# Loading the first block of tokens in two halves, one on each DMA queue

## The chip, the core and the metric

The kernel runs on one core of a Trainium2 chip. A core has five engines with instruction queues of their own: TensorE (matmuls; PE in the profile), VectorE (DVE), ScalarE (ACT), GpSimd (POOL) and SyncE (SP). SyncE and ScalarE also issue the transfers between the chip's main memory (HBM) and the on-chip memory (SBUF); matmul results go to PSUM, from where VectorE or ScalarE must copy them before their bank can be used again. The metric is the device time of one execution in microseconds (us), the median of several.

## What is computed

One transformer layer with two branches in parallel: attention over a window of 256 keys with 32 heads of 16 channels, and a bilinear feed-forward part. Both read the same layer norm of x; x is 2048 tokens by 512 channels in bf16.

```python
def _A_ref(x, wqkv, wo):
    H = 32; Dh = D // H; W = 256
    qkv = transpose((x @ wqkv).reshape(B, S, 3, H, Dh), 2, 0, 3, 1, 4)
    q, k, v = qkv[0], qkv[1], qkv[2]
    scores = jnp.einsum("bhqd,bhkd->bhqk", q, k) * (Dh ** -0.5)
    mask = (idx[:, None] - idx[None, :] >= 0) & (idx[:, None] - idx[None, :] < W)
    p = _softmax(jnp.where(mask[None, None], scores, -1e9), axis=-1)
    return transpose(jnp.einsum("bhqk,bhkd->bhqd", p, v), ...).reshape(B, S, D) @ wo

def _B_ref(x, w_gate, w_up, w_down):
    h = jnp.einsum("bsd,df->bsf", x, w_gate) * jnp.einsum("bsd,df->bsf", x, w_up)
    return jnp.einsum("bsf,fd->bsd", h, w_down)

xn = _layernorm(x, axis=-1)
return x + _A_ref(xn, A_wqkv, A_wo) + _B_ref(xn, B_w_gate, B_w_up, B_w_down)
```

## The kernel before

The tokens are cut into 16 blocks of 128 (x0 to x15) and the work into four chunks of four blocks. A planner in the kernel's own Python code decides, while the program is built, in which order the pieces of work are put on the engines. It is given constants for how long each piece takes, and for when each load is expected to land (`land` for the blocks of x, `wv`, `wk`, `wq` for the thirds of Wqkv). These constants do nothing on the chip: they only set the order, and which of two engines takes a copy.

The loads are issued at the head of the program:

```python
def qkv(eng, lo, k0, k1):     # 512 of the 1536 columns of Wqkv, rows k0 to k1 of 4 slices of 128
    load(eng, self.Wqkv[:, k0:k1, lo:lo + 512], w["qkv"][:, k0:k1, lo:lo + 512])

load(nc.scalar, self.x[:, 0, :], xv[:, 0, :])
load(nc.sync, self.x[:, 1, :], xv[:, 1, :])
qkv(nc.sync, 1024, 0, 2)      # V weights, k 0,1
qkv(nc.scalar, 1024, 2, 4)    # V weights, k 2,3
qkv(nc.scalar, 512, 2, 4)     # K weights, k 2,3
qkv(nc.sync, 512, 0, 2)       # K weights, k 0,1
load(nc.sync, self.x[:, 2, :], xv[:, 2, :])
qkv(nc.sync, 0, 0, 4)         # Q weights
load(nc.sync, self.x[:, 3, :], xv[:, 3, :])
# ... then, all on nc.sync: Wg and Wu in halves, x4 to x7, x8 to x15
for f, g in ((0, 5), (5, 10), (10, 14)):
    load(nc.sync, self.Wd[:, f:g], w["d"][:, f:g])
load(nc.sync, self.Wo[:], w["o"])
for _ in range(4):
    nc.sync.drain()
# ... small constants; a Sqrt of one element on ScalarE brings in its table:
nc.scalar.activation(out=warm[:], in_=warm[:], func=ACT.Sqrt)
# ...
for _ in range(4):
    nc.vector.drain()
self.keep_busy(42, 0)         # 42 matmuls of 128 columns on constants
```

The first chunk, block by block (b = 0 to 3), with what each step needs:

```python
land = (3.35, 3.4, 7.5, 9.6)
wv, wk, wq = 5.6, 6.9, 9.2
# st{b}: bn_stats and bn_aggr of x[b]          VectorE, after the load of x[b]
# sq{b}: sqrt(var + eps)                       ScalarE
# rs{b}: reciprocal                            VectorE
# ap{b}: xn[b] = (x - mean) * rs               VectorE, block 0 in two halves of 256 channels
def turn(i, ks, b=b):                        # TensorE: four 128x128 transposes into PSUM
    for k in ks:
        self.nc.tensor.transpose(self.psT(i)[:, k, :], self.xn[b][:, 128 * k:128 * k + 128], self.ident[:])
    if b == 0:
        self.keep_busy(2 * ks[0], 3)
# xT{b}: copy to xnT[0] in SBUF                ScalarE or VectorE
def project(i, lo, tok=tok):                 # K (lo = 512) and Q (lo = 0) of one block: 16 matmuls
    for k in range(4):
        for c in range(4):
            self.nc.tensor.matmul(
                self.M[i][:, 128 * c:128 * c + 128], lhsT=self.Wqkv[:, k, lo + 128 * c:lo + 128 * c + 128],
                rhs=self.xnT[0][:, k, tok], start=k + c == 0, stop=k == 3, skip_group_check=True)
# V of one block: 16 matmuls too; then the copies out of PSUM (K in two, Q and V in one)
```

TensorE works in the order it is given. In the first chunk that is: the 42 matmuls, the transposes of block 0, V of block 0, the transposes of block 1, K of block 0, K of block 1, Q of block 0, the transposes of block 2, and so on; then the feed-forward part, the scores and the values in turns until the end.

Of the kernel before, what the change touches and what calls it, by code (L numbers as in the profile page):

```python
# [90 lines left out]
class Kernel:  # L91
# [58 lines left out]
    def prologue(self):  # L150
        nc = self.nc
        xv = self.x_d.rearrange("(t p) d -> p t d", p=128)
        w = {k: v.rearrange("(k p) n -> p k n", p=128) for k, v in self.w_d.items()}

        def load(eng, dst, src):
            eng.dma_start(out=dst, in_=src)

        def qkv(eng, lo, k0, k1):
            load(eng, self.Wqkv[:, k0:k1, lo:lo + 512], w["qkv"][:, k0:k1, lo:lo + 512])

        load(nc.scalar, self.x[:, 0, :], xv[:, 0, :])
        load(nc.sync, self.x[:, 1, :], xv[:, 1, :])
        qkv(nc.sync, 1024, 0, 2)
        qkv(nc.scalar, 1024, 2, 4)
        qkv(nc.scalar, 512, 2, 4)
        qkv(nc.sync, 512, 0, 2)
        load(nc.sync, self.x[:, 2, :], xv[:, 2, :])
        qkv(nc.sync, 0, 0, 4)
        load(nc.sync, self.x[:, 3, :], xv[:, 3, :])
        h = self.F // 2  # L170
        for lo in (0, h):
            load(nc.sync, self.Wg[:, :, lo:lo + h], w["g"][:, :, lo:lo + h])
            load(nc.sync, self.Wu[:, :, lo:lo + h], w["u"][:, :, lo:lo + h])
            if lo == 0:
                load(nc.sync, self.x[:, 4:8, :], xv[:, 4:8, :])
        load(nc.sync, self.x[:, 8:NT, :], xv[:, 8:NT, :])
        for f, g in ((0, 5), (5, 10), (10, 14)):
            load(nc.sync, self.Wd[:, f:g], w["d"][:, f:g])
        load(nc.sync, self.Wo[:], w["o"])
        for _ in range(4):  # L180
            nc.sync.drain()

        c = self.const
        nc.gpsimd.memset(self.ident[:], 0.0)
        nc.gpsimd.affine_select(out=self.ident[:], in_=self.ident[:], compare_op=ALU.not_equal, fill=1.0,
                                base=0, pattern=[[-1, 128]], channel_multiplier=1)
        nc.gpsimd.memset(self.mhalf[:], -0.5)
        warm = c.tile([128, 1], F32, name="warm")
        nc.vector.memset(warm[:], 0.0)
        nc.vector.memset(self.eps[:], 1e-5)  # L190
        nc.scalar.activation(out=warm[:], in_=warm[:], func=ACT.Sqrt)
        self.warm = warm
        pi = c.tile([128, 1], I32, name="pi")
        nc.gpsimd.iota(pi[:], pattern=[[0, 1]], base=0, channel_multiplier=1)
        podd = c.tile([128, 1], I32, name="podd")
        nc.vector.tensor_scalar(out=podd[:], in0=pi[:], scalar1=4, scalar2=1,
                                op0=ALU.arith_shift_right, op1=ALU.bitwise_and)
        nc.vector.tensor_copy(out=self.own[:, 1:2], in_=podd[:])
        nc.vector.tensor_scalar(out=self.own[:, 0:1], in0=podd[:], scalar1=0, scalar2=None, op0=ALU.is_equal)
        nc.gpsimd.memset(self.V[0][:, :, :, 16:18], 1.0)  # L200
        for _ in range(4):
            nc.vector.drain()
        self.keep_busy(42, 0)


# [385 lines left out]

    def first_chunk(self):

        land = (3.35, 3.4, 7.5, 9.6)
        wv, wk, wq = 5.6, 6.9, 9.2
        nc = self.nc
        roots = []
        for b in range(4):
# [36 lines left out]
        for b in range(4):  # L635
# [40 lines left out]
            for n, ks in enumerate(([0, 1], [2, 3]) if b == 0 else ([0, 1, 2, 3],)):  # L676
                self.A.insert(at + n, Dense(f"turn{b}", 1.1 * len(ks) / 4, [("ap", b, n)], lambda i, f=turn, ks=ks: f(i, ks),
                                            lambda o, i, f=turned, ks=ks: f(o, i, ks)))
# [172 lines left out]
```

The softmax here doesn't subtract the row's maximum and nothing guards it: scores larger than these inputs give would overflow.

## Time and profile before

| what | value |
|---|---|
| time, median of 3 | 264.75 us (264.62 to 264.78) |
| profiled execution | 903.53 us, span 901.7 us |
| TensorE busy | 897.7 us of the span |
| ScalarE, VectorE, GpSimd busy | 168.1, 195.0, 118.1 us |
| HBM read and written | 9.70 and 2.10 MB |

In the profiled execution TensorE worked far more slowly than in the timed ones (42 matmuls of 128 columns take 8.67 us at its head), so its durations are not those of the 264.75 us; the times of loads, VectorE and ScalarE do not hang on TensorE's speed except where they wait for it. A line of a timeline reads: start, duration, engine (q for the queue that issues a transfer), source line, operation, output <- input, how many, and in brackets the idle time before it and what ended it. A line of the DMA view gives output <- input, issuing queue, count, size of one, and us from issue to landing.

### The profile page before, as it was taken

Reading aid. Unit: us, or ns where it says so; the run is one execution under the profiler, and the core shown is the slowest. Engines: PE = TensorE matmul, PEld = TensorE weight load, DVE = VectorE, ACT = ScalarE, POOL = GpSimd, SP = SyncE. Lnnn points to the kernel's source line nnn. Section 1 sums busy time; section 2 is a strip of 40 time slices with the busy share of each in tenths; the row PEclk is TensorE's granted clock in tenths of the full one; section 3 lists DMA queues with packets and bytes.
Section 4 is the critical chain, followed back from the end, with each engine's and each line's share of the span. In section 5 each row is a group of like instructions: output and inputs, shape, how many; then the busy total and the mean of one; then the engine's idle time right before and its main releaser. Section 6 shows DMA issues by size and latency. Waiting matters only on the chain.

```text
span 901.7 us, 8001 instructions
## 1 busy us (share of the span) xinstructions
PE 897.7 (100%) x3456; PEld 290.7 (32%) x3456; DVE 195.0 (22%) x367; ACT 168.1 (19%) x122; POOL 118.1 (13%) x274
## 2 busy tenths in 40 slices
PE   9999999999999999999999999999999999999998
PEld 8832223523222222343222222324323232322333
DVE  2132222222222021312222021312202022222101
ACT  2221112222112121121121211111212121120000
POOL 0112111210212011110212011110110202011000
DMA  9301000000001000000000000000000000000000
GB/s 328 104 0 24 0 1 1 0 1 1 1 6 24 12 7 0 1 1 1 0 18 19 6 7 0 1 1 1 1 4 8 6 1 7 1 0 0 1 1 24
DMA packets 17252, 13.89 MB, mean 15 GB/s; under 512 B 7104, under 2 KB 17216, under 8 KB 17216
## 3 DMA queue, kind: packets, MB, share of 16 engines
q1 hardware_dynamic: 16384, 12.65, 4.7%
q10 hardware_dynamic: 832, 0.72, 0.2%
q8 instruction: 27, 0.44, 0.2%
q14 instruction: 9, 0.07, 0.0%
HBM read 9.70 MB, written 2.10 MB: 13 GB/s over the span
## 4 chain that ended last, share of the span: by engine, by line
PE 100%; DVE 0%; issue 0%; DVEq 0%
PE M L221 75%; PE S L229 7%; PE M L259 7%; PE M L707 6%; PE M L655 3%; PE M L211 1%; PE S L221 1%; PE M L640 0%; DVE xn L801 0%; DVEq L801 0%
## 5 line engine op out<-in xcount | busy, mean ns | idle before, releaser
L512 ACT ACTIVATE P<-S 128x2048 bf16<-128x2048 f32 x75 | 140.8, 1877 | 459.0 <-PE S L229 452.7
L238 POOL TENSOR_SCALAR_AFFINE_SELECT P<-P 64x256 bf16<-64x256 bf16 (+1 forms) x250 | 111.0, 446 | 673.9 <-ACT P L512 662.8
L221 PE MATMUL M<-xnT,Wu 128*128 128x512 bf16 x224 | 197.7, 1114 | 0.0
L221 PE MATMUL M<-xnT,Wg 128*128 128x512 bf16 x224 | 194.0, 1056 | 0.0
L221 PE MATMUL M<-Wd,hT 128*128 128x512 bf16 (+1 forms) x224 | 181.9, 1056 | 0.0
L221 PEld LDWEIGHTS <-Wg 128*128 128x128 bf16 x224 | 44.4, 204 | 119.1 <-issue 119.1
L221 PEld LDWEIGHTS <-Wu 128*128 128x128 bf16 x224 | 42.5, 197 | 121.9 <-issue 121.9
L221 PEld LDWEIGHTS <-hT 128*128 128x128 bf16 x238 | 45.2, 198 | 112.7 <-issue 112.1
L221 PE MATMUL M<-xnT,Wqkv 128*128 128x512 bf16 x96 | 79.8, 1085 | 0.0
L759 DVE TENSOR_TENSOR hT<-M,gsb 128x512 bf16<-128x512 f32 x56 | 38.7, 691 | 172.8 <-PE M L221 172.8
L229 PE MATMUL S<-Q,K 32*128 32x320 bf16 (+4 forms) x720 | 67.9, 532 | 0.0
L259 PE MATMUL M<-P,V 64*17 64x320 bf16 (+4 forms) x1440 | 62.1, 591 | 0.0
L217 DVE CAST gsb<-M 128x512 bf16<-128x512 f32 x44 | 30.4, 691 | 139.5 <-PE M L221 139.5
L229 PEld LDWEIGHTS <-K 32*128 32x128 bf16 x720 | 16.4, 115 | 122.5 <-issue 121.7
L221 PE MATMUL M<-Wo,OT 128*128 128x512 bf16 (+1 forms) x64 | 53.8, 1070 | 0.0
L707 PE MATMUL M<-Wqkv,xnT 128*64 128x256 bf16 x256 | 53.1, 670 | 0.0
L259 PEld LDWEIGHTS <-V 64*17 64x17 bf16 x1440 | 42.2, 188 | 22.2 <-issue 18.0
L550 DVE STREAM_TRANSPOSE at<-M 128x512 f32<-128x512 f32 x32 | 21.5, 699 | 85.3 <-PE M L259 85.3
L707 PEld LDWEIGHTS <-xnT 128*64 128x64 bf16 x256 | 33.9, 209 | 18.6 <-issue 10.8
L801 DVE TENSOR_TENSOR y<-M,x 128x512 bf16<-128x512 f32 x12 | 8.3, 691 | 121.0 <-PE M L221 121.0
L221 PEld LDWEIGHTS <-Wqkv 128*128 128x128 bf16 x96 | 18.1, 196 | 50.8 <-issue 50.8
L655 PE MATMUL M<-xnT,Wqkv 128*128 128x128 bf16 x128 | 27.2, 484 | 0.0
(53 smaller groups left out, 211.7 us busy)
## 6 DMA issues: line engine op xcount, KB each, us to landing
Wg<-in_B_w_gate_dram SPq DMA_DIRECT2D x2, 896.0 KB, 9.5
Wu<-in_B_w_up_dram SPq DMA_DIRECT2D x2, 896.0 KB, 11.3
out_dram<-y SPq DMA_DIRECT2D x12, 128.0 KB, 1.7
Wd<-in_B_w_down_dram SPq DMA_DIRECT2D x2, 640.0 KB, 12.9
x<-in_A_x_dram SPq DMA_DIRECT2D x1, 1024.0 KB, 14.3
Wqkv<-in_A_wqkv_dram ACTq DMA_DIRECT2D x2, 256.0 KB, 5.2
Wqkv<-in_A_wqkv_dram SPq DMA_DIRECT2D x2, 256.0 KB, 4.8
Wqkv<-in_A_wqkv_dram SPq DMA_DIRECT2D x1, 512.0 KB, 6.7
```

The lines of the kernel that those rows point to most:

```text
L211: self.nc.tensor.matmul(self.M[i][:, 0:128], lhsT=ones, rhs=ones, start=True, stop=True)
L217: self.nc.vector.tensor_copy(out=out, in_=in_)
L221: self.nc.tensor.matmul(ps, lhsT=a, rhs=b, start=first and n == 0, stop=last and n == len(pairs) - 1)
L229: self.nc.tensor.matmul(self.S[:, e, 64 * at:64 * (at + m)], lhsT=self.K[U % 3][rows, c, j].rearrange("p l t -> p (l t)"), rhs=self.Q[T % ...
L238: self.nc.gpsimd.affine_select(out=v, in_=v, pattern=[[0, 4], [0, n], [sign, 64]], base=0, fill=0.0, compare_op=ALU.is_gt if kind else ALU ...
L259: self.nc.tensor.matmul(banks[lane][32 * e:32 * e + 17, 64 * q:64 * (q + m)], lhsT=self.V[U % 3][rows, j, 4 * c + e, 0:17], rhs=P[rows, e, ...
L512: ex = self.op(f"exp{g}", {"A": (took + 0.06, took + 0.18)}, [o], lambda e: self.nc.scalar.activation(out=P[:, :, 0:hi], in_=self.S[:, :, ...
L550: t = self.op(f"tr{v}", {"V": (0.63, 0.71)}, [o] + ts, lambda e, par=par: nc.vector.transpose(out=self.at[:, :, par, :], in_=self.M[banks[ ...
L655: self.nc.tensor.matmul(self.M[i][:, 128 * c:128 * c + 128], lhsT=self.Wqkv[:, k, lo + 128 * c:lo + 128 * c + 128], rhs=self.xnT[0][:, k, ...
L707: self.nc.tensor.matmul(self.M[i][64 * lane:64 * lane + 64, 256 * jj:256 * jj + 256], lhsT=self.xnT[T % 2][:, k, tok], rhs=w[:, lane], sta ...
L759: x = self.op(f"u{T}.{f}", {"V": PSUM_COPY["V"]}, [o, ("gate", T, f)], lambda e: self.nc.vector.tensor_tensor(out=self.hT[T % 2][:, f, :], ...
L801: self.nc.vector.tensor_tensor(out=keep["y"][:, cols], in0=self.M[i][:, cols], in1=self.x[:, t, cols], op=ALU.add)
```

## The change

The first block of x, which everything else waits for, is cut into two halves of 64 tokens (64 partitions). Each of the two queues that issue loads starts with one half, so that no other load stands ahead of x0 or beside it. The load of x1, which stood at the head of SyncE's queue, goes behind the half of x0 on ScalarE's queue, ahead of the weights. The other loads keep their order; Wd is loaded in two parts, not three; three of four drains of VectorE are left out. The planner is given new landing times to match.

```diff
-        load(nc.scalar, self.x[:, 0, :], xv[:, 0, :])
-        load(nc.sync, self.x[:, 1, :], xv[:, 1, :])
+        load(nc.sync, self.x[0:64, 0, :], xv[0:64, 0, :])
+        load(nc.scalar, self.x[64:128, 0, :], xv[64:128, 0, :])
+        load(nc.scalar, self.x[:, 1, :], xv[:, 1, :])
         qkv(nc.sync, 1024, 0, 2)
         qkv(nc.scalar, 1024, 2, 4)
         qkv(nc.scalar, 512, 2, 4)
@@
-        for f, g in ((0, 5), (5, 10), (10, 14)):
+        for f, g in ((0, 7), (7, 14)):
             load(nc.sync, self.Wd[:, f:g], w["d"][:, f:g])
@@
-        for _ in range(4):
-            nc.vector.drain()
+        nc.vector.drain()
         self.keep_busy(42, 0)
@@
-        land = (3.35, 3.4, 7.5, 9.6)
-        wv, wk, wq = 5.6, 6.9, 9.2
+        land = (3.25, 3.9, 7.7, 9.7)
+        wv, wk, wq = 5.9, 7.3, 9.4
```

## The prediction

> **What bounds the kernel now.** I read the page's busy shares and chain first. The profiled execution is 901.7 us long against 264.75 us timed, so the first question is which of its numbers may be used.
>
> ```profile
> span 901.7 us, 8001 instructions
> ...
> PE 897.7 (100%) x3456; PEld 290.7 (32%) x3456; DVE 195.0 (22%) x367; ACT 168.1 (19%) x122; POOL 118.1 (13%) x274
> ...
> DMA  9301000000001000000000000000000000000000
> ...
> PE 100%; DVE 0%; issue 0%; DVEq 0%
> ```
>
> The chain of work is TensorE from end to end, so here every wait of the head is hidden behind a slow TensorE. In the chain in order of time, 48 projection matmuls of 128 columns take 9.77 us, 204 ns each. Timed, all of 901.7 us of such work has to fit in 264.75 - (903.53 - 901.7) = 262.9 us, so TensorE is at least 3.4 times faster there. I therefore take TensorE's order from the profile, but not its durations. Durations of VectorE, ScalarE and the transfers I take as they stand. The DMA row matters next: it is busy in the first two slices (45 us) and then nearly nothing, so this change can act on the head alone.
>
> The timeline of the first 6 us, from issue of the loads to the first normalised tile (start, duration, engine and line, what ended the wait):
>
> ```profile
> 0.80 0.41 ACTq L156 DMA_DIRECT2D x<-in_A_x_dram  x1
> ...
> 0.80 0.40 SPq L156 DMA_DIRECT2D x<-in_A_x_dram  x1
> ...
> 2.28 1.28 ACT L191 ACT_TABLE_LOAD   x1 [2.28 <-issue]
> ...
> 3.58 0.20 ACT L191 ACTIVATE warm<-warm 128x1 f32<-128x1 f32 x1
> ...
> 3.61 0.69 DVE L607 BATCH_NORM_STATS2 st<-x 128x6 f32<-128x512 bf16 x1 [1.67 <-DMA x<-in_A_x_dram]
> ...
> 4.33 0.18 DVE L609 BATCH_NORM_AGGREGATE mv<-st 128x2 f32<-128x6 f32 x1
> ...
> 4.55 0.29 ACT L616 ACTIVATE ve<-mv,eps 128x1 f32<-128x1 f32 x1 [0.77 <-DVE mv L609]
> ...
> 4.88 0.16 DVE L619 RECIPROCAL rs<-ve 128x1 f32<-128x1 f32 x1
> 5.08 0.60 DVE L287 TENSOR_SCALAR xn<-x,mv,rs 128x256 bf16<-128x256 bf16 x2
> ```
>
> The only wait on a load in it is VectorE's, 1.67 us for x0. From landing at 3.6 to the first half of xn0 at about 5.38 (5.08 plus half of 0.60) there is nothing but this chain. The transfers, from the DMA view cut to short windows (size, us from issue to landing):
>
> ```profile
> x<-in_A_x_dram ACTq DMA_DIRECT2D x1, 128.0 KB, 2.8
> x<-in_A_x_dram SPq DMA_DIRECT2D x1, 128.0 KB, 2.6
> ...
> Wqkv<-in_A_wqkv_dram ACTq DMA_DIRECT2D x1, 256.0 KB, 4.5
> Wqkv<-in_A_wqkv_dram SPq DMA_DIRECT2D x1, 256.0 KB, 4.0
> ...
> Wqkv<-in_A_wqkv_dram SPq DMA_DIRECT2D x1, 256.0 KB, 5.7
> Wqkv<-in_A_wqkv_dram ACTq DMA_DIRECT2D x1, 256.0 KB, 6.0
> ...
> Wqkv<-in_A_wqkv_dram SPq DMA_DIRECT2D x1, 512.0 KB, 6.7
> ```
>
> With the issue times of the timeline (0.80; 1.23 and 1.26; both 1.73; 2.74) the landings before are: x1 3.4, x0 3.6; V weights 5.3 (k 0,1) and 5.7 (k 2,3); K weights 7.4 and 7.7; Q weights 9.4. From the same views x2 lands at 2.23 + 5.7 = 7.9 and x3 at 3.60 + 6.2 = 9.8. The stretches show 57 GB/s in 1.5 to 2.0 us, 188 in 2.0 to 2.5, 320 in 2.5 to 3.0, then 281, 367 and 326 in the three whole microseconds from 3 to 6: from 2.5 us on the queues are full, and whatever is put ahead delays what stands behind.
>
> **What the Trainium skill says.** "DMA: Bandwidth & Descriptors", section Rules for kernel authors, advises against two transfers to disjoint partition halves, since both spread over the same 16 engines. The section Issuing engines are not separate DMA queues adds that several issuers save sequencer time only. The trace agrees with the sharing: two 128 KB loads issued together on two queues landed within 0.2 us of each other. "TensorE: Matmul & The Clock Gate", Part 1, gives 107 ns for a 128-column matmul cold and 56 ns warm; this trace shows 204 ns instead, so the two figures serve for estimates of the timed run only. "ScalarE: Activation LUTs", section What ACT_TABLE_LOAD costs, gives 1283 ns; the trace has 1.28 us.
>
> **The change, part by part.**
>
> (a) x0 sooner. Before, x0 and x1 share the engines, so x0 is complete after about 256 KB. After, both queues carry a half of x0 and it is complete after 128 KB. From the stretches, 0.5 x 57 + 0.5 x 188 = 122 KB have moved by 2.5 us, and the next 128 KB at 320 GB/s need 0.4 us. So x0 may land up to 0.4 us sooner, near 3.2. Two things cap this. ScalarE now issues four loads ahead of its table load, not three, at some 0.45 us each, so the table load ends at 2.28 + 0.45 + 1.28 = 4.0 and the warm-up at 4.2, where the square root now begins at 4.55: at most 0.35 us of gain can pass. And the transposes stand behind 42 warm-up matmuls: 0.84 + 42 x 0.107 = 5.3 us cold (estimate from the TensorE page), and earlier if the clock rises in them; xn0 is there at 5.38 now. I put the gain at the first transpose at 0.2 us (0.05 to 0.35).
>
> (b) x1 later. It lands behind 64 KB more of x0 on its own queue and beside the V weights: roughly 3.9. Its first statistics run at 4.43 now, so it costs nothing.
>
> (c) V and K weights of ScalarE's queue later. That queue carries 64 + 128 KB ahead of V where it carried 128; with fair sharing the other queue moves 64 KB more in the time too, so 128 KB at 325 GB/s (mean of 281, 367, 326) = 0.4 us. V k 2,3: 5.7 to 6.1. K k 2,3: 7.7 to 8.1. The SP halves come sooner by as much: V 4.9, K 7.0. Q weights, x2 and x3: the sum of bytes ahead is the same, so unchanged to +0.1.
>
> (d) TensorE's order. Leaving bank numbers aside, the new arrival times handed to the planner move one thing: the four transposes of xn3 go ahead of one projection of 16 matmuls rather than behind it. Four copies out of PSUM in the first chunk change engine (one of the two of K of block 0 and xnT of block 2 go to VectorE, Q of block 0 goes to ScalarE and Q of block 1 to VectorE); each is 0.60 to 0.69 us and lies beside TensorE.
>
> (e) Three drains fewer on VectorE fall in its idle 1.93 to 3.61 us; two Wd loads for three end long before the first use. Both nothing.
>
> Now the head of TensorE at timed speed, estimating 0.9 us per 16-matmul projection (16 x 56 ns) and 0.25 per transpose group. Before: transposes 5.4, their copies (0.38 and 0.29) end at 6.3, V projection 6.3 to 7.2, xn1's transposes to 7.45, first K projection from 7.45 (its k 2,3 half landed at 7.7 just in time) to 8.4, second K to 9.3, Q projection at 9.4 when its weights land. After: V projection 6.1 to 7.0, transposes to 7.25, K on its first half to 7.7, then a wait for the other half until 8.1, end 8.55, second K 9.45, Q at 9.45 to 9.5. The gain of 0.2 is lost at the K weights, and the Q weights set the same point in both. Net by then 0 to +0.1 us. The xn3 transposes follow at 9.5 + 0.9 + 0.25 + 0.9 = 11.55; xn3 itself needs x3 at 9.8 plus 0.69 + 0.18 + 0.28 + 0.16 + 0.41 and hand-overs of some 0.25, 11.8: a new wait of 0.25 us, which before lay behind one more projection. Sum: between -0.2 and +0.4, middle +0.1 us on 264.75. TensorE is the bound after this, so the difference reaches the end undiminished.
>
> **Rivals.** First, the K and Q weights do not bind in the timed run (transfers beside a profiled TensorE may be slower than otherwise); then the 0.1 to 0.35 us of (a) stay and the time is 264.4 to 264.65. For it: slack before the V projection is 0.6 us. Against it: 7.7 and 9.4 us fall right on the computed starts. Second, the ScalarE queue is worse off than fair sharing says, the V half lands beyond 6.4 and each K half waits again: +0.3 to +0.7, 265.0 to 265.5. For it: the planner's new arrival times move V, K and Q later by 0.2 to 0.4 and x0 earlier by only 0.1. Third, the banks handed out from the xn3 transposes on are different for the whole kernel, so later evictions could meet other hand-overs; the order of the work is the same, so I allow 0.3 us either way.
>
> **Range and chances.** Mechanism +0.1, its spread 0.3 each way, the third rival another 0.3, the spread of the times before 0.16: predicted 264.8 us, range 264.2 to 265.5 for 8 in 10. Two per cent are 5.3 us, more than ten times any term above: within 2% 0.98, faster 0.01, slower 0.01.
>
> **What would show it.** In the profile after: x0's statistics start near 3.2 rather than 3.61, table load 0.45 later, the landing of K's ScalarE half near 8.1, its SP half near 7.0, Q's unchanged at 9.4. I am wrong if x0 lands at most 0.1 sooner, if Q's weights move by over 0.2, or if the time moves by over 0.8 us, which only the later order could explain.

## The result, and the profile after

The changed kernel takes 265.81 us (median of 5 runs, 265.28 to 266.28) against 264.75 us: 1.0038 times the time before, 95% interval 1.0022 to 1.0055. It is slower by 1.06 us, below 2%, and outside the predicted range of 264.2 to 265.5.

The profile of the changed kernel, page lines that answer to those of before:

```profile
span 264.5 us, 7964 instructions
...
PE 256.7 (97%) x3421; PEld 132.3 (50%) x3456; DVE 190.7 (72%) x369; ACT 164.5 (62%) x120; POOL 119.2 (45%) x274
...
DMA  6999920000001300000003300000000100000002
...
PE 90%; DMA 3%; ACT 2%; DVE 2%; issue 1%; ACTq 0%
```

TensorE works at its timed speed here and is busy for 97% of the span; the chain still lies on it. The DMA row is at 0.6 to 0.9 in the first five slices of 6.6 us and then nearly empty. This profile cannot be laid beside the 901.7 us profile of before, so the kernel before was profiled again (first experiment, "the control"); its span at the timed speed is 263.0 us. All comparisons below are with the control.

The head of the changed kernel, from its timeline (start, duration, engine and line, what ended the wait):

```profile
0.80 0.58 SPq L156 DMA_DIRECT2D x<-in_A_x_dram  x1
0.80 1.19 ACTq L156 DMA_DIRECT2D x<-in_A_x_dram  x2
...
1.44 1.34 SPq L156 DMA_DIRECT2D Wqkv<-in_A_wqkv_dram  x2
...
2.03 0.98 ACTq L156 DMA_DIRECT2D Wqkv<-in_A_wqkv_dram  x2
...
3.69 0.69 DVE L607 BATCH_NORM_STATS2 st<-x 128x6 f32<-128x512 bf16 x1 [1.75 <-DMA x<-in_A_x_dram]
...
6.02 0.63 PE L211 MATMUL M<-const-bfloat16-1.0 128*128 128x128 bf16 x4
...
6.58 0.63 PE L707 MATMUL M<-Wqkv,xnT 128*64 128x256 bf16 x8
...
7.74 0.63 PE L707 MATMUL M<-Wqkv,xnT 128*64 128x256 bf16 x8 [0.54 <-DMA Wqkv<-in_A_wqkv_dram]
...
12.92 0.40 PE L640 MATMUL M<-ident,xn 128*128 128x128 bf16 x4 [0.28 <-DVE xn L287]
```

The control, same view:

```profile
1.23 1.02 ACTq L156 DMA_DIRECT2D Wqkv<-in_A_wqkv_dram  x2
...
3.65 0.69 DVE L607 BATCH_NORM_STATS2 st<-x 128x6 f32<-128x512 bf16 x1 [1.71 <-DMA x<-in_A_x_dram]
...
5.91 0.39 PE L211 MATMUL M<-const-bfloat16-1.0 128*128 128x128 bf16 x4
...
6.29 1.06 PE L707 MATMUL M<-Wqkv,xnT 128*64 128x256 bf16 x16
...
12.39 0.39 PE L640 MATMUL M<-ident,xn 128*128 128x128 bf16 x4
```

Read the lines in pairs. x0's statistics start at 3.69 where they started at 3.65: x0, given both queues to itself, is not there sooner (and its transposes start at 5.57 and 5.53). The issue of ScalarE's V half moved from 1.23 to 2.03. The V projection, 16 matmuls in one go at 6.29 before, is broken in two after: eight at 6.58, then a wait for weights, eight at 7.74. And xn3's transposes, which found their operand ready at 12.39, now wait 0.28 us for VectorE.

V's first matmul is 0.29 us later although the transposes are only 0.04 later; the loads account for those 0.04 alone. The four transposes and the four matmuls on constants behind them took 0.65 and 0.63 us; in the control they took 0.54 and 0.39. TensorE starts at a slow pace in every profile but the first (which has one still slower), one 128-column matmul every 0.107 us, and goes over to one every 0.059 us at a moment that differs between executions. The 42 matmuls at its head, the same in all kernels, took 3.99 us in the control, 4.64 in the changed kernel (the slow pace throughout), and between 3.83 and 4.64 in the others.

The landings after, from the DMA view cut to the issues between 1.8 and 2.1 us:

```profile
Wqkv<-in_A_wqkv_dram SPq DMA_DIRECT2D x1, 256.0 KB, 4.8
Wqkv<-in_A_wqkv_dram ACTq DMA_DIRECT2D x1, 256.0 KB, 5.7
```

ScalarE's V half: 2.03 + 5.7 = 7.7, which is when the second half of V starts. In the control the same half lands at 1.23 + 4.2 = 5.4. How the queues filled is in the stretches of one microsecond; the last column is GB/s, the one before it the DMA share. Control:

```profile
3.00:4.00 1.00, 1.00 (x13) 1.00 (x11) 0.35 (x1) 0.77 (x2) 0.00 (x0) 1.00 0.95 303
4.00:5.00 1.00, 0.83 (x14) 0.65 (x12) 0.92 (x4) 0.29 (x1) 0.00 (x0) 1.00 1.10 376
```

Changed kernel:

```profile
3.00:4.00 1.00, 1.00 (x13) 1.00 (x11) 0.30 (x1) 0.97 (x1) 0.00 (x0) 1.00 0.76 195
4.00:5.00 1.00, 1.00 (x12) 1.00 (x11) 0.91 (x4) 0.81 (x3) 0.00 (x0) 1.00 0.97 285
```

In the stretches from 1 to 2 and from 2 to 3 us it is 19 and 221 GB/s against 0 and 154. By 5 us the control has moved 19 + 221 + 303 + 376 = 919 KB, the changed kernel 634: 285 KB less, or 0.8 us at some 360 GB/s. So the head did not merely deal the same bytes out differently; fewer bytes moved. But that alone does not put V at 7.7. In the profile of e1_loads_old_order below, with the same loads, 0 + 162 + 186 + 292 = 640 KB had moved by 5 us, and ScalarE's V half landed at 2.00 + 4.2 = 6.2. The trace records a landing in sixteen parts: in the changed kernel fifteen parts of this half are there by 6.44 us and the last one at 7.70, in e1_loads_old_order all sixteen by 6.16. Why one part came so late is open.

From about 11.5 us on, TensorE's k-th weight load is later than in the control by a constant, within 0.05 us, up to the last: 1.42 to 1.43 us in this profile, whose execution took 266.28 us, the slowest of the five. That "lag" of TensorE against the control, worked out from the start times in the two traces, is given for the experiments too. Here it builds up in steps: 0.04 at x0's transposes, 0.29 at V (the slow pace), 0.97 behind V (the wait for weights) and 1.43 behind xn3's transposes. It belongs to one execution; verdicts rest on the medians.

### The profile page after: what moved, and what is told of

It reads as the page before. It is cut to its first block, busy times and chain, and to the rows that moved or that the text cites. A ratio compares the mean times of both kernels' runs of the same rounds, so it can differ in the third digit from the quotient of the medians.

```text
span 264.5 us, 7964 instructions
## 1 busy us (share of the span) xinstructions
PE 256.7 (97%) x3421; PEld 132.3 (50%) x3456; DVE 190.7 (72%) x369; ACT 164.5 (62%) x120; POOL 119.2 (45%) x274
## 4 chain that ended last, share of the span: by engine, by line
PE 90%; DMA 3%; ACT 2%; DVE 2%; issue 1%; ACTq 0%
PE M L221 66%; PE S L229 9%; PE M L259 7%; PE M L707 6%; DMA Wqkv<-in_A_wqkv_dram 2%; ACT P L512 1%; PE M L655 1%; DMA out_dram<-xn 1%; PE S L221 1%; DVE xn L801 1%; DVE st L607 0%; ACTq L156 0%; ACT Q L215 0%; DVE xn L287 0%; DVE V L217 0%
## 5 line engine op out<-in xcount | busy, mean ns | idle before, releaser
L221 PE MATMUL M<-xnT,Wg 128*128 128x512 bf16 x218 | 57.3, 380 | 0.4
L221 PE MATMUL M<-xnT,Wu 128*128 128x512 bf16 x213 | 56.8, 380 | 0.5
L221 PE MATMUL M<-Wd,hT 128*128 128x512 bf16 (+1 forms) x213 | 50.2, 373 | 1.4 <-issue 1.3
L221 PEld LDWEIGHTS <-hT 128*128 128x128 bf16 x238 | 21.3, 98 | 23.0 <-issue 2.7
L229 PE MATMUL S<-Q,K 32*128 32x320 bf16 (+4 forms) x720 | 29.9, 254 | 0.3
L550 DVE STREAM_TRANSPOSE at<-M 128x512 f32<-128x512 f32 x32 | 21.4, 699 | 11.5 <-PE M L259 11.4
L221 PE MATMUL M<-xnT,Wqkv 128*128 128x512 bf16 x91 | 22.3, 380 | 0.3
L259 PE MATMUL M<-P,V 64*17 64x320 bf16 (+4 forms) x1440 | 19.5, 252 | 0.0
L259 PEld LDWEIGHTS <-V 64*17 64x17 bf16 x1440 | 17.0, 86 | 2.6 <-issue 0.8
L707 PE MATMUL M<-Wqkv,xnT 128*64 128x256 bf16 x256 | 15.7, 274 | 0.5 <-DMA Wqkv<-in_A_wqkv_dram 0.5
L221 PE MATMUL M<-Wo,OT 128*128 128x512 bf16 (+1 forms) x62 | 15.4, 373 | 0.2 <-issue 0.2
```

Source lines behind the costliest of these rows:

```text
L221: self.nc.tensor.matmul(ps, lhsT=a, rhs=b, start=first and n == 0, stop=last and n == len(pairs) - 1)
L229: self.nc.tensor.matmul(self.S[:, e, 64 * at:64 * (at + m)], lhsT=self.K[U % 3][rows, c, j].rearrange("p l t -> p (l t)"), rhs=self.Q[T % ...
L259: self.nc.tensor.matmul(banks[lane][32 * e:32 * e + 17, 64 * q:64 * (q + m)], lhsT=self.V[U % 3][rows, j, 4 * c + e, 0:17], rhs=P[rows, e, ...
L550: t = self.op(f"tr{v}", {"V": (0.63, 0.71)}, [o] + ts, lambda e, par=par: nc.vector.transpose(out=self.at[:, :, par, :], in_=self.M[banks[ ...
L707: self.nc.tensor.matmul(self.M[i][64 * lane:64 * lane + 64, 256 * jj:256 * jj + 256], lhsT=self.xnT[T % 2][:, k, tok], rhs=w[:, lane], sta ...
```

## The experiments

There are three places to look: the loads (64-partition halves that issue and start more slowly, or ScalarE's weights standing behind two loads), TensorE's order (the wait at xn3), and something outside the head (renamed banks, the drains, the end of the program). The expectations name theories by letters: V, the late V weights cost it; O, the order costs it; H, the shape of the halves makes the loads slow; Q, the place in the queue does; A, the number of instructions on an engine makes the end stall; N, it does not.

### The control

base_again: the kernel before, unchanged.

> The kernel before, unchanged, to have its profile with TensorE at the speed of the timed runs (the first profile had it at less than a third). Time 264.75 within 0.2. If the loads' issue times come out as in the first profile (0.40 to 0.52 us each, V weights landed by 5.7 us), the 0.56 to 0.67 us and the V landing at 7.7 us in the changed kernel belong to the change; if they come out near 0.6 here too, they belong to the faster execution and not to the change.

Measured: 264.74 us, 1.0000 (0.9992 to 1.0008). Its first loads take 0.40 to 0.52 us to issue. The 0.58 us of the changed kernel belong to the change.

### Which part costs: loads or order

e1_loads_old_order: the changed kernel with the planner's old numbers, so the new loads (with the change's drains and Wd) in the old order.

```diff
-        land = (3.25, 3.9, 7.7, 9.7)
-        wv, wk, wq = 5.9, 7.3, 9.4
+        land = (3.35, 3.4, 7.5, 9.6)
+        wv, wk, wq = 5.6, 6.9, 9.2
```

> The changed loads (with the drains and Wd of the change), but the planner is given the old landing times, so the order of work is that of before. Theory V (the V weights on ScalarE's queue land later, third behind two x loads, and TensorE waits for them in the first V projection): all of the loss stays, 265.5 to 266.1. Theory O (the order is what costs: xn3's transposes ahead of a projection and other banks): back to 264.6 to 264.9. If both, in between: the wait of 0.28 us before xn3's transposes goes, 265.5.

Measured: 265.23 us (264.61 to 266.28, 22 runs), 1.0020 (1.0011 to 1.0028). In its profile x0 did come early:

```profile
3.28 0.69 DVE L607 BATCH_NORM_STATS2 st<-x 128x6 f32<-128x512 bf16 x1 [1.34 <-DMA x<-in_A_x_dram]
```

Its transposes started at 5.33, 0.20 us before the control's, V did not wait for weights, and K then waited for its half on ScalarE's queue:

```profile
8.15 2.38 PEld L655 LDWEIGHTS <-Wqkv 128*128 128x128 bf16 x40 [0.24 <-DMA Wqkv<-in_A_wqkv_dram]
```

The lag was 0.16 us only. The same program in other executions took up to 266.28 us. So the loads cost 0.4 to 0.5 us (0.4 between the medians, 264.82 for the kernel before beside it; 0.5 by the ratio), and from nothing to 1.5 us in a single execution.

e2_order_old_loads: the reverse, the kernel before (four drains) with the planner's new numbers.

```diff
-        land = (3.35, 3.4, 7.5, 9.6)
-        wv, wk, wq = 5.6, 6.9, 9.2
+        land = (3.25, 3.9, 7.7, 9.7)
+        wv, wk, wq = 5.9, 7.3, 9.4
```

> The loads, drains and Wd of before, but the planner is given the new landing times, so TensorE's order is that of the changed kernel. Theory V: 264.5 to 265.0, at most the 0.28 us wait before xn3's transposes. Theory O: 265.5 to 266.1.

Measured: 266.35 us (266.21 to 266.61), 1.0056 (1.0044 to 1.0068), slower than the whole change. The timeline at xn3:

```profile
11.85 0.40 PE L640 MATMUL M<-ident,xn 128*128 128x128 bf16 x4 [0.21 <-DVE xn L287]
```

The lag is -0.02 us before it and 0.36 to 0.37 from there to the last weight load. The rest came after the last matmul: from TensorE's last weight load to the end it is 4.56 us, 3.38 in the control. Two lines show it, the last addition on VectorE, and the last output from the DMA view. The control:

```profile
260.07 0.42 DVE L801 TENSOR_TENSOR xn<-S,x 128x256 bf16<-128x256 f32 x1
```
```profile
out_dram<-xn ACTq DMA_DIRECT2D x1, 64.0 KB, 1.6
```

e2_order_old_loads:

```profile
260.81 0.42 DVE L801 TENSOR_TENSOR xn<-S,x 128x256 bf16<-128x256 f32 x1 [0.29 <-issue]
```
```profile
out_dram<-xn ACTq DMA_DIRECT2D x1, 64.0 KB, 2.4
```

The addition waits for nothing that is recorded ("issue"), and the output then takes 0.8 us longer. Counted in the traces, with those of its sequencer, VectorE has 452 instructions in e2_order_old_loads, 450 both before and after. I suspected that the count decides this end, and took two drains out.

h1_order_two_drains: e2_order_old_loads with two drains fewer, 450 instructions again.

```diff
-        for _ in range(4):
+        for _ in range(2):
             nc.vector.drain()
```

> The new order on the old loads again, with two VectorE drains fewer, so that VectorE has as many instructions as in the kernel before and in the changed one (two fewer than in the run of the new order with four drains, which took 266.35). Theory A (of the 1.6 us there, 0.37 is the wait ahead of xn3's transposes and the rest is a stall at the end that comes with VectorE's instruction count): 265.0 to 265.3, and the time after the last weight load back from 4.56 to 3.4 us. Theory O (the order as such costs 1.5 us): 266.2 to 266.5 as before.

Measured: 265.36 us (264.96 to 265.94, 12 runs), 1.0019 (1.0011 to 1.0027), 1.0 us less than e2_order_old_loads; the end takes some 3.4 us again and the last output lands in 1.6. The wait at xn3 is 0.34 us in this run, the lag 0.57. So the order costs about 0.5 us, and in this program two drains of VectorE cost about 1.0 us at the end. All five profiles with the new order show the step of the lag at xn3's transposes: 0.45 us in the changed kernel, 0.32 to 0.55 in the others.

The two parts add up: 1.0020 x 1.0019 = 1.0039, measured 1.0038 for the change.

### The end of the program and the drains

g1_after_four_drains: the changed kernel with all four drains (453 instructions on VectorE).

```diff
-        nc.vector.drain()
+        for _ in range(4):
+            nc.vector.drain()
         self.keep_busy(42, 0)
```

> The changed kernel with the four VectorE drains of before (three instructions more on VectorE). Theory A ([...]with two instructions more than before, the new order on the old loads ended with VectorE idle for 0.29 us before the last addition and output landings of 2.4 instead of 1.6 us): 0.7 to 1.2 us slower than the changed kernel, 266.5 to 267.0, all of it after the last matmul. Theory N (the drains lie in idle time and cost nothing): 265.8 within 0.3.

Measured: 266.18 us (265.71 to 266.44), 1.0043 (1.0031 to 1.0055). The end took 3.53 us: no stall, though the count is higher than in e2_order_old_loads. So a count above 450 does not by itself make the stall; which counts do is open. Its head showed something else:

```profile
5.49 0.43 DVE L608 BATCH_NORM_STATS2 st<-x 128x6 f32<-128x256 bf16 x1 [1.34 <-DMA x<-in_A_x_dram]
5.83 0.15 DVE L620 RECIPROCAL rs<-ve 128x1 f32<-128x1 f32 x1
```

x0's statistics were done at 3.97 + 0.18 = 4.15 us here, but x1's first statistics stand ahead of x0's reciprocal in VectorE's order. With x1 late, x0 waits behind it: TensorE was idle for 1.38 us there (0.69 in the control). The lag is 0.76 before xn3's transposes and 1.31 behind them.

### x1 behind x0

e3_x1_behind_v: the changed kernel with the load of x1 behind the V weights.

```diff
-        load(nc.scalar, self.x[:, 1, :], xv[:, 1, :])
         qkv(nc.sync, 1024, 0, 2)
         qkv(nc.scalar, 1024, 2, 4)
+        load(nc.scalar, self.x[:, 1, :], xv[:, 1, :])
```

> The changed kernel with one line moved: x1 goes behind the V weights on ScalarE's queue, so that V k 2,3 is second in its queue and not third. Theory V: V k 2,3 is issued some 0.6 us sooner and lands by 6.9 us or before, the wait of 0.54 us in the first V projection goes, and the time falls by 0.4 to 0.9 to some 265.1, unless x1, which lands later then (some 4.5 us), becomes the wait instead. Theory O: unchanged within 0.2 of 265.8.

Measured: 268.84 us, 1.0146 (1.0133 to 1.0159).
V k 2,3 came early, as Theory V said, but x1 became the wait: its first statistics start at 5.97 after a wait of 1.57 us, x0's reciprocal behind them. The lag is 4.2 us, more than the wait, since the V projection then took 1.92 us for its 16 matmuls where the control took 1.06, and the 48 projections after it 4.24 us where the control took 2.98. TensorE was at its slow pace there: its 42 first matmuls had taken 4.64 us, so it had not gone over to the fast one before it fell idle.

f3_x1_on_sync: the changed kernel with x1 behind the half on SyncE's queue, old order, three drains and Wd in three parts.

```diff
-        load(nc.scalar, self.x[:, 1, :], xv[:, 1, :])
+        load(nc.sync, self.x[:, 1, :], xv[:, 1, :])
@@
-        for f, g in ((0, 7), (7, 14)):
+        for f, g in ((0, 5), (5, 10), (10, 14)):
@@
-        nc.vector.drain()
+        for _ in range(3):
+            nc.vector.drain()
@@
-        land = (3.25, 3.9, 7.7, 9.7)
-        wv, wk, wq = 5.9, 7.3, 9.4
+        land = (3.35, 3.4, 7.5, 9.6)
+        wv, wk, wq = 5.6, 6.9, 9.2
```

> Halves of 64 tokens at both heads, but x1 goes behind the half on SyncE's queue and not on ScalarE's; planner numbers of before, three drains. Theory H: first issues still 0.56 to 0.67, first bytes after 2.0 us, and now V k 0,1 is the late half (SyncE's third): TensorE waits at the start of the first V projection, 265.0 to 265.8. Theory Q as stated (ScalarE's queue alone is the trouble): V k 2,3 second there, 264.6 to 264.9.

Measured: 266.21 us (265.81 to 268.05), 1.0065 (1.0042 to 1.0087). V started at 6.22 after a wait of 0.28 us for weights, as Theory H expected, yet the lag is 0.09 us only. The end takes 4.31 us, with the last SyncE output issued 0.42 us late. SyncE has 90 instructions here, 89 in the control.

h2_x1_on_sync_sp_drain: f3_x1_on_sync with one of SyncE's drains left out (89 instructions).

```diff
-        for _ in range(4):
+        for _ in range(3):
             nc.sync.drain()
```

> Halves of 64 tokens, x1 behind the half on SyncE's queue, as the run that took 266.21, with one SyncE drain fewer, so that SyncE has as many instructions as before. Its profile had TensorE only 0.09 us late but the end 4.31 us after the last weight load, not 3.4. Theory A: the end is back at 3.4 us and the time at 264.8 to 265.3, with first issues still near 0.58 us. If the count has nothing to do with it: 266 or more.

Measured: 265.52 us (265.07 to 267.38, 13 runs), 1.0035 (1.0019 to 1.0052), above what was expected. The end is back at 3.4 us. In the profiled run, at 266.88 us, x1's statistics waited 1.02 us, V took 1.92 us and the lag was 2.04. So x1 can be late on either queue; its place on ScalarE's alone is not the cause.

The issue times go with it. In all six profiles with a 64-partition half at both heads, the load right behind a half is slow to issue too: on one queue it takes 0.82 to 0.85 us, on the other 0.56 to 0.60. Where the slower of the two was x1 (g1_after_four_drains and this run), x1 landed at 5.5 and 5.2 us; where it was V (the changed kernel, e1_loads_old_order, f3_x1_on_sync), x1 landed at 3.8 to 4.0. The same loads can go either way.

### The shape of the halves

f2_halves_by_channel: x0 in halves of 128 tokens by 256 channels, in the same places; order, drains and Wd edited as in f3_x1_on_sync.

```diff
-        load(nc.sync, self.x[0:64, 0, :], xv[0:64, 0, :])
-        load(nc.scalar, self.x[64:128, 0, :], xv[64:128, 0, :])
+        load(nc.sync, self.x[:, 0, 0:256], xv[:, 0, 0:256])
+        load(nc.scalar, self.x[:, 0, 256:512], xv[:, 0, 256:512])
```

> As the changed loads in the old order, but x0 is cut by channels, not tokens: each half is 128 partitions of 512 bytes, 64 KB. Three drains on VectorE keep its instruction count. Theory H in the form that the number of partitions of the halves slows the issue: issue times back at 0.4 to 0.5 us and 264.5 to 264.9. If any cut into two small loads does it, or the place in the queue: as the changed loads, issues near 0.58 and 265.0 to 265.5.

Measured: 264.93 us, 1.0002 (0.9994 to 1.0010), no loss. The issues in its timeline:

```profile
0.80 0.90 ACTq L156 DMA_DIRECT2D x<-in_A_x_dram  x2
...
0.81 0.40 SPq L156 DMA_DIRECT2D x<-in_A_x_dram  x1
```

A half takes 0.40 us to issue, not 0.58, for the same 64 KB on the same queue, and V follows on ScalarE at 1.73 rather than 2.03. x1 and V behind the halves take 0.46 and 0.42 us. x0 was not early either: its statistics started at 4.22 us, and the lag of this one execution is 0.44. By 5 us 31 + 103 + 233 + 360 = 727 KB had moved, also fewer than in the control. What this run shows is that the loss goes with the 64-partition shape; that the shorter issues are the reason is likely, but not shown.

f1_x0_whole: the kernel before with x0 whole on ScalarE's queue and x1 behind it, so that SyncE starts with V.

```diff
-        load(nc.sync, self.x[:, 1, :], xv[:, 1, :])
+        load(nc.scalar, self.x[:, 1, :], xv[:, 1, :])
```

> The kernel before (its planner numbers, drains and Wd) with one thing of the change: x1 moved from the head of SyncE's queue to behind x0 on ScalarE's; x0 stays whole. Theory H (the two 64-partition halves are what makes the first issues cost 0.56 to 0.67 us instead of 0.41 to 0.5 and the first bytes move after 2.0 us instead of 1.5): issues are back at 0.4 to 0.5, the V weights land by 6.2 us, the time is 264.5 to 264.9. Theory Q (what costs is the third place of the V weights in ScalarE's queue, with or without halves): V k 2,3 still lands after 6.3 us in most runs and the time is 265.0 to 265.6, as with the changed loads in the old order (265.23).

Measured: 265.02 us, 1.0016 (0.9998 to 1.0033). x0's statistics start at 3.36 and its transposes at 5.31, 0.2 us before the control's, with no half at all; but V follows at 6.32 (6.29 in the control), and a K half makes TensorE wait:

```profile
8.47 2.23 PEld L655 LDWEIGHTS <-Wqkv 128*128 128x128 bf16 x40 [0.28 <-DMA Wqkv<-in_A_wqkv_dram]
```

So x0 sooner by 0.3 us bought nothing here: the slow pace took the head start (transposes and constants 0.65 and 0.63 us, as in the changed kernel), and then the weights came too late. The lag is 0.33.

h3_x1_in_halves: the kernel before with x1, not x0, in two 64-token halves on SyncE's queue, and one drain fewer on each of VectorE and SyncE to keep 450 and 89.

```diff
-        load(nc.sync, self.x[:, 1, :], xv[:, 1, :])
+        load(nc.sync, self.x[0:64, 1, :], xv[0:64, 1, :])
+        load(nc.sync, self.x[64:128, 1, :], xv[64:128, 1, :])
```

> The kernel before with x0 whole at the head of ScalarE's queue, as it was, and x1 in two halves of 64 tokens at the head of SyncE's (instruction counts kept). Theory H, own queue: SyncE's two half issues cost near 0.58 us each, ScalarE's stay at 0.41. Theory H, shared: ScalarE's rise too. x1 lands later (some 3.9 us) but still ahead of its statistics at 4.48, and V k 0,1 is issued 0.7 us later: 264.7 to 265.3.

Measured: 265.46 us (264.77 to 267.54, 12 runs), 1.0031 (1.0011 to 1.0052), above what was expected. Its timeline:

```profile
0.80 0.39 ACTq L156 DMA_DIRECT2D x<-in_A_x_dram  x1
...
0.80 1.21 SPq L156 DMA_DIRECT2D x<-in_A_x_dram  x2
...
3.08 0.69 DVE L608 BATCH_NORM_STATS2 st<-x 128x6 f32<-128x512 bf16 x1 [1.13 <-DMA x<-in_A_x_dram]
...
5.14 0.43 DVE L608 BATCH_NORM_STATS2 st<-x 128x6 f32<-128x256 bf16 x1 [1.15 <-DMA x<-in_A_x_dram]
```

The two halves take 1.21 us on their own queue, and the other queue's issue stays at 0.39. The whole x0 on ScalarE, with the other queue slow to start, is there at 3.08, earlier than in any other profile of this study. That x1 would land by 3.9 was a miss: its statistics start at 5.14, and x0's transposes, behind them, at 6.07.

### A better version

k1_x0_whole_k_balanced: f1_x0_whole with K's weights cut k 0 to 2 on SyncE and k 3 on ScalarE, to remove its wait at K.

```diff
-        qkv(nc.scalar, 512, 2, 4)
-        qkv(nc.sync, 512, 0, 2)
+        qkv(nc.scalar, 512, 3, 4)
+        qkv(nc.sync, 512, 0, 3)
```

> The run with x0 whole and x1 behind it on ScalarE's queue (265.02, with x0's statistics at 3.36 and not 3.65, but a wait of 0.28 us for K k 2,3), with one change: K is cut in k 0 to 2 on SyncE's queue and k 3 on ScalarE's, so that both queues carry 640 KB up to the end of K. If the K wait is what eats x0's gain: the wait goes and 264.4 to 264.7, as fast as the kernel before or 0.2 faster. If not, 264.9 to 265.2.

Measured: 265.19 us (264.41 to 267.44, 14 runs), 1.0013 (0.9997 to 1.0029). In the profiled run, 264.74 us, the wait at K is gone and the lag is -0.03, but x0's statistics start at 3.55 in it. In the median it does not beat the kernel before, and no version here did.

## Why the prediction was wrong

The figure was 264.8 and the time is 265.81. Two terms of the sum failed. "Net by then 0 to +0.1 us", for the loads up to the Q projection, took every load to land when its bytes are due; measured, the loads cost 0.4 to 0.5 us, because V's weights or x1 land later than that in some executions. And the order, taken as a wait of 0.25 us at xn3, costs 0.5 us. All three signs of being wrong that the prediction named came: x0 landed no sooner (3.60 us in the changed kernel's profile), Q's weights moved by 1.0, and the time by 1.06.

**(a) x0 sooner: right in some executions only.** The step counted bytes: 128 KB instead of 256 ahead of x0, hence up to 0.4 us. It assumed that a 64-partition half issues and starts like the 128-partition load it replaces. The issue took 0.58 us instead of 0.40, and nothing moved before 2 us (19 GB/s in the control). x0's statistics started at 3.69 in the changed kernel's profile, at 3.28 with the same loads in e1_loads_old_order and at 3.25 in g1_after_four_drains, against 3.65. In e1_loads_old_order the cap that the step named held as well: x0's reciprocal came at 4.73 instead of 4.92, behind the square root, and the transposes 0.20 us sooner, the very gain predicted. In f2_halves_by_channel, same bytes and places but 128 partitions, the loss is gone (1.0002 against 1.0020 for e1_loads_old_order, intervals that do not overlap; the two differ in drains and Wd as well, but both ends take 3.4 us). The prediction quoted the Trainium skill, "DMA: Bandwidth & Descriptors", Rules for kernel authors, against partition halves and then priced them as free; the advice held, and these traces add to it a longer issue and a later start.

**(b) x1 later: failed.** "It costs nothing" needed x1 by about 4.4 us. When it lands later, VectorE's order makes x0's reciprocal wait for it. With x1 in the change's place that was a wait of 1.34 us in g1_after_four_drains; with x1 in other places 1.02, 1.15 and 1.57 us (h2_x1_on_sync_sp_drain, h3_x1_in_halves, e3_x1_behind_v). In the profiles of the changed kernel and of e1_loads_old_order x1 was there in time (landed at 3.99 and 3.83), so there the step did no harm; it is a risk of some executions.

**(c) The V and K weights: right in one execution, far too small in another.** Predicted: V k 2,3 by 0.4 to 6.1, K k 2,3 to 8.1 with a wait of TensorE there, SyncE's V half earlier at 4.9, Q unchanged at 9.4. In e1_loads_old_order they land at 6.2, 8.1 (TensorE waits), 5.5 and 9.6: all but SyncE's V half within 0.2 of what was said, and the lag is 0.16. In the changed kernel's profile they land at 7.7, 2.51 + 6.4 = 8.9, 1.44 + 4.8 = 6.2, and 3.33 + 7.1 = 10.4. The shortfall of 285 KB by 5 us does not explain the difference, since e1_loads_old_order has nearly the same (279 KB). TensorE's wait of 0.54 us inside V, 0.68 of the lag, comes from the last of sixteen parts of one load.

**(d) The order: right mechanism, under-sized by half.** Predicted a new wait of 0.25 us; 0.28 is recorded as idle in the changed kernel's profile, but the lag steps up by 0.45 there, by 0.38 in e2_order_old_loads and by 0.51 in h1_order_two_drains, whose median is 0.5 us up. The prediction also summed it badly: its own terms, 0 to +0.1 by Q and +0.25 at xn3, add to 0.25 to 0.35, and it wrote a middle of +0.1.

**(e) Drains and Wd: net right, for a reason the step did not have.** The end takes 3.45 us, 3.38 in the control. But the drains are not free to add or leave out: with the new order, four of them cost 1.0 us more than two. The change leaves three out, and VectorE's count stays at 450. What stalls there is open; g1_after_four_drains, at 453, does not fit a simple threshold.

**The rivals.** The first (K and Q do not bind, a gain) fell. The second was nearest: ScalarE's V half beyond 6.4, +0.3 to +0.7. It happened in the changed kernel's profile (7.7) and not in that of e1_loads_old_order (6.2), and it lacked the second part from the order. The third, renamed banks costing 0.3, is refuted for this profile: the lag is constant within 0.05 us from 11.5 us to the last weight load, so nothing after the head adds or gives back. "Reaches the end undiminished" held, and "over 0.8 us, which only the later order could explain" did not: the order gave half.

**Left open.** Why the same program's loads land 0.5 us or more apart between executions (264.61 to 266.28 us in e1_loads_old_order); how the changed kernel's 0.4 to 0.5 us of loads divides between the late weights of (c) and the late x1 of (b), since each profile shows one execution; whether the moment at which TensorE takes up its fast pace has anything to do with the loads, since 42 first matmuls of 4.64 us occur with the old loads too (h1_order_two_drains); and what makes the end stall.

## What to carry to other kernels

Cutting a small first load by partitions over two queues is not halving its time: look at the issue time and at when the first bytes move. Here the cut by channels (within a partition) brought no loss clear of noise, and no gain either. A load that is moved back is free only if no instruction ahead of the critical one in its consumer's order waits for it. Time a change of load order and of instruction order separately and repeat each, because one profile of a load-bound head can show anything from no loss to the whole loss.

## What the runs showed of the hardware

- Loads of 64 partitions x 512 channels of bf16 took 0.55 to 0.58 us to issue, 128 x 256 ones of the same 64 KB 0.40 to 0.41, on their own queue only (0.39 beside them on the other, h3_x1_in_halves). The load right behind such a half took 0.56 to 0.85 us; behind a 128-partition load it took 0.41 to 0.47.
- With 64-partition halves at both heads no byte moved before 2.1 us; in the control the first moved at 1.8.
- The sixteen parts of one 256 KB load landed between 5.37 and 7.70 us, fifteen of them by 6.44 (changed kernel, ScalarE's V half).
- Two drains more on VectorE at the head cost 1.0 us at the end (266.35 against 265.36 us), and one drain more on SyncE lengthened the end from 3.4 to 4.3 us; three more on VectorE in the changed kernel did not (3.53 us).
- TensorE's first 42 matmuls took 3.83 to 4.64 us, by the moment at which its pace went from 0.107 to 0.059 us each. Where it had changed before TensorE fell idle, 1.38 and 1.43 us of idle time did not undo it: 16 V matmuls took 1.06 us (g1_after_four_drains, f2_halves_by_channel, with 4.21 and 3.83 us for the 42). Where it had not (4.64 us), V took 1.92 us after 1.42 and 0.70 us of idle time (e3_x1_behind_v, h2_x1_on_sync_sp_drain).
